# Second block of an attention and two-MLP kernel: the second weight tile's conversion queued on ScalarE behind the silu of tile (1,1)

## The chip, the cores and the metric

The kernel runs on one core of a Trainium2 chip. The metric is the device time of one execution in microseconds (us). Before the change three runs gave 1042.11, 1042.42 and 1044.66 us; the median is 1042.42 us.

## The reference

Three stages follow each other, all in float32 from outside:

```python
scores = scale * q @ k.T + (cum[:, None] - cum[None, :])   # causal, 4 batches x 8 heads x 576 rows x 64
x = softmax(scores) @ v                                    # reshaped to 2304 tokens x 512
xn = x / sqrt(mean(x * x) + 1e-6) * rms_g                  # first block
x = (silu(xn @ w_gate) * (xn @ w_val)) @ w_out             # 512 -> 1536 -> 512
h = x @ w_in                                               # second block
out = (silu(h)) @ w_out2                                   # 512 -> 2048 -> 512
```

`cum` is the running sum of log(f). The change touches the second block alone: `h = x @ w_in`, silu, and the product with `w_out2`.

## The kernel before, in words

**Numbers.** Every float32 operand of a large product is split into a high part (what ScalarE writes when it copies the value to the type fp32r, `hi`) and the rest (`lo`, value minus high part, computed on VectorE or GpSimd). A product is then three matmuls: high by high, low by high, high by low.

**Stages.** Attention comes first, then `layer("a", ...)` (the first block) for the first 1280 tokens and for the other 1024, then `layer("b", ...)` (the second block) for the same two parts, which the text calls the first and the second part of the second block. A layer walks over its inner dimension in groups of two 128-wide chunks (`for g in range(0, NF, G)`); the second block has eight groups in each part, called group 1 to group 8 here. In the first part they begin, with the first matmul that reads the operand `b11`, at 650.77, 674.75, 700.79, 728.35, 756.30, 782.40, 809.65 and 835.70 us of the profiled execution; the second part begins some 26 us after the last of these.

**One group.** Two chunks times two times 512 tokens make a 2 by 2 product that is computed with seven products instead of eight (the scheme of Winograd and Strassen). `Products` holds them: `p1` to `p7`, run in the order p1, p2, p6, p5, p7, p4, p3. Weight operands are `a11, a12, a21, a22` (pieces of the weights) and `s1` to `s4` (sums and differences of them); token operands are `b11, b21, b22` and `t1` to `t4`. Products p1, p6, p7 and p4 go to one PSUM bank, `u`, in which they accumulate. In between, ScalarE copies the bank out (`copy`, L731, tiles `c<-t`): after p1, after p6 and after p7. So p4's matmuls (`t<-t4h,wh` in the rows) can't start before the copy behind p7 is done. `plus` (L736, VectorE) adds a PSUM bank to such a copy. In the first part there is also a remainder of 256 tokens (`rest`).

Output tiles of a group are named by (chunk, token column). (1,1) is ready first after the seventh product, p7: copy of `u`, `plus`, then `out_` is called, which issues the silu (L829, ScalarE) and the split of its result into `hh` (L638, ScalarE) and `hl` (L639, VectorE). Then come the remainder's two tiles, (1,0) (behind p4) and (0,1) (behind p3). `hh` and `hl` are what the second product of the block (with `w_out2`) reads. That product is not run in its own group but in the next one: `second2` makes blocks of six matmuls, and the next group runs one or two of them behind each of its own products. Their PSUM tiles are `x` and `s`, and VectorE adds each to the result `xa` (L896).

**Weights of the second block.** `unit_in` (line 148) prepares a group's input weights while the group before it runs. Two tiles `f[0]` and `f[1]` come by DMA; GpSimd makes the four sums and differences (L162, `f<-f`, four instructions); ScalarE converts each tile to its high part (L165, `wh<-f`); the low part (L166, `wl<-f,wh`) is made by VectorE for the first tile, and for the second tile by GpSimd in the first part and by VectorE in the second part. The first tile holds a11, a12, s1 and s2 (for p1, p2, p6, p5), the second a21, a22, s3 and s4 (for p7, p4, p3).

```python
for i in range(2):
    u = slice(0 if plain or not i else 1, 4)
    nc.scalar.activation(out=hi[i][:, u], in_=f[i][:, u], func=AF.Copy)
    (nc.gpsimd if plain and i else nc.vector).tensor_tensor(out=lo[i][:, u], in0=f[i][:, u], in1=hi[i][:, u].bitcast(F32), op=ALU.subtract)
```

`plain` is true in the first part here. The weights arrive as 64-bit floats. In the first part the raw tile `st` is loaded (SyncE queue, L141) and unpacked to float32 by one ScalarE instruction (L143) and four of VectorE (L144 to L147), and the result is stored to DRAM (`kept`, L149) for the second part, which loads it ready-made (L134). Eight of the sixteen input tiles (those of groups 1, 2, 7 and 8) were unpacked during the first block; those of groups 3 to 6 are unpacked while groups 2 to 5 run. The output weights (`unit_out`, L193 on ScalarE and L194 on GpSimd, tiles `woh` and `wol`) are unpacked in every group of the first part. In groups 3 and 4 GpSimd also forms differences of the second part's tokens (L650).

**Order of the work.** A scheduler orders every engine's queue when the program is built, by readiness and priority; an engine then takes its queue strictly in order. `spread` (line 697) holds a unit back with `tc.issue_after(after)`: what is traced inside is queued on `after`'s engine somewhere behind the instruction `after`, without waiting for its end. For a unit of the second block `after` is one of the first silus of the group before (`marks`, `LEAD`).

Of the kernel before, what the change touches and what calls it, by code (L numbers as in the profile page):

```python
# [13 lines left out]
AF = mybir.ActivationFunctionType  # L14
# [47 lines left out]
def block_kernel(ctx: ExitStack, tc: tile.TileContext, q, k, v, f, w_gate, w_val, w_o1, rms_g, w_in, w_o2, ident_d, sel_d, hot_d, out):  # L62
    nc = tc.nc
# [56 lines left out]
    def plain_half():  # L120
        return stp.tile([P, 4, G2], F32, tag="f", name="f", bufs=3)

    def words(w):
        return (w, 1) if w.dtype == F32 else (w.bitcast(I32), 2)
# [26 lines left out]
    def unit_in(w, key, m, plain):  # L151


        w, s = words(w)
        hi, lo = zip(*((wip.tile([P, 4, G2], F32R, tag="wh", name="wh"), wip.tile([P, 4, G2], F32R, tag="wl", name="wl")) for _ in range(2)))
        f = [plain_half() for _ in range(2)]
        for i in range(2):
            weights(f[i][:, :2].rearrange("p a f -> p (a f)"), w[:, s * (m + i) * P : s * (m + i + 1) * P], s * P, (key, m + i))
        a11, a12, a21, a22 = f[0][:, 0], f[0][:, 1], f[1][:, 0], f[1][:, 1]
        s1, s2, s3, s4 = f[0][:, 3], f[0][:, 2], f[1][:, 2], f[1][:, 3]  # L160
        for out_, x, y, op in ((s1, a21, a22, ALU.add), (s2, s1, a11, ALU.subtract), (s3, a11, a21, ALU.subtract), (s4, a12, s2, ALU.subtract)):
            nc.gpsimd.tensor_tensor(out=out_, in0=x, in1=y, op=op)  # L162
        for i in range(2):
            u = slice(0 if plain or not i else 1, 4)
            nc.scalar.activation(out=hi[i][:, u], in_=f[i][:, u], func=AF.Copy)  # L165
            (nc.gpsimd if plain and i else nc.vector).tensor_tensor(out=lo[i][:, u], in0=f[i][:, u], in1=hi[i][:, u].bitcast(F32), op=ALU.subtract)  # L166
        ops = lambda i, b: tuple(t[i][:, b].rearrange("p (c f) -> p c f", f=P) for t in (hi, lo))
        return dict(a11=ops(0, 0), a12=ops(0, 1), s2=ops(0, 2), s1=ops(0, 3), a21=ops(1, 0), a22=ops(1, 1), s3=ops(1, 2), s4=ops(1, 3))
# [468 lines left out]
    def split(hi, lo, src):  # L637
        nc.scalar.activation(out=hi, in_=src, func=AF.Copy)  # L638
        nc.vector.tensor_tensor(out=lo, in0=src, in1=hi.bitcast(F32), op=ALU.subtract)  # L639
# [71 lines left out]
        with tc.issue_after(after):  # L711
            return fn(*args)

    places, marks, pending, done = [], [], [], [0]

    def terms(ps, abs_, start, stop):
        mms = [(a[i], b[j]) for a, b in abs_ for i, j in ((0, 0), (0, 1), (1, 0))]
# [91 lines left out]
    def layer(n, w_ins, w_out, second, ph, plain=False, ahead=()):  # L809
        NF = w_out.shape[0] // P  # L810
        in_fours[:] = [] if len(w_ins) == 2 and not plain else [True]
        G = 2
        for g in range(0, NF, G):
            win = [spread(*((unit_plain, w, f"{n}{z}", g) if plain else (unit_in, w, f"{n}{z}", g, ph == 0))) for z, w in enumerate(w_ins)]
            wout = [spread(unit_out, w_out, f"{n}o", m) for m in range(g, g + G)]
            for fn in ahead[g // G] if ahead else ():
# [8 lines left out]
            def out_(z, at_, a, w):  # L825
                psum_ = plain or at_ == (1, 0) or at_[1] == 2
                if z == 0:
                    hf = tmp.tile([P, TT], F32, tag="c", name="c")[:, :w] if psum_ else a
                    act = nc.scalar.activation(out=hf, in_=a, func=AF.Silu)  # L829
                    marks.append(act.ins)  # L830
                    if len(w_ins) == 2:
                        gates[at_] = hf
                        return
                else:
                    hf = gates[at_]
                    (nc.vector if psum_ or at_ == (0, 1) else nc.gpsimd).tensor_tensor(out=hf, in0=a, in1=hf, op=ALU.mult)  # L836
                few = dict(tag="r", bufs=2) if w < TT else dict(tag="h", bufs=5)
                hh, hl = (hp_.tile([P, w], F32R, tag=few["tag"] + p, name="h" + p, bufs=few["bufs"]) for p in "hl")
                split(hh, hl, hf)
                hs[at_] = hh, hl  # L840

            todo, pending[:] = list(pending), []
            order = group(win, out_, ph == 0, plain)

            if plain and coming:
# [110 lines left out]
```

## Time and profile before

| | us |
|---|---|
| median of the runs shown | 1042.42 |
| the profiled execution's own time | 1045.11 |
| its span | 1043.3 |
| TensorE (PE) busy in the span | 1023.5 (98%) |
| VectorE (DVE) busy | 763.2 (73%) |
| ScalarE (ACT) busy | 565.8 (54%) |
| GpSimd (POOL) busy | 411.8 (39%) |

The profile is one execution. The profiled execution took 2.69 us more than the median of the runs, and its span is 1.81 us shorter than its own time. All times in the rows are counted from the span's start. The granted clock of TensorE was 1.00 of full speed in every stretch of the second block, which is the 2.4 GHz level. "Busy" of TensorE is modelled, so it is not a sign of peak speed. A wait is named after the instruction that ended last before the waiting one could go on.

### The profile page before, as it was taken

To read this page: it belongs to the slowest core of one execution; us is meant where nothing else is said; L and a number is where in the kernel's file an instruction comes from. 1 tells how busy PE (TensorE), PEld (TensorE's weight loads), DVE (VectorE), ACT (ScalarE), POOL (GpSimd) and SP (SyncE) were. 2 spreads that over 40 slices of the span, in tenths; PEclk is the share of its full clock that TensorE was granted. 3 is DMA by queue.
4 is the path that set the end of the run, shared out by engine and by line. 5 is a ranking of instruction groups with operands and counts; after the bars stand their busy time and mean duration, and the time that the engine had idled before them with its cause. 6 is when DMAs were issued, how large, how long until landed. Compare 5 with 4: busy or idle time off the path is not lost.

```text
span 1043.3 us, 16043 instructions
## 1 busy us (share of the span) xinstructions
PE 1023.5 (98%) x5459; PEld 846.2 (81%) x5459; DVE 763.2 (73%) x1509; ACT 565.8 (54%) x1191; POOL 411.8 (39%) x601
## 2 busy tenths in 40 slices
PE   8999999999999999999999999999999999999998
PEld 7876777878788888888787787887788888888886
DVE  6889887877666767976478667968886696366664
ACT  6998988883442322543544455664454465544441
POOL 8786766511111216332355635235544323222300
PEclk8999999999999999999999999999999999999999
DMA  6564543113432424230433222134442233111102
GB/s 145 133 183 123 138 107 92 36 62 104 139 106 77 158 84 152 71 112 31 122 112 127 97 61 71 61 122 152 151 152 82 81 121 135 48 61 61 51 1 81
DMA packets 113010, 104.30 MB, mean 100 GB/s; under 512 B 62769, under 2 KB 83665, under 8 KB 112929
## 3 DMA queue, kind: packets, MB, share of 16 engines
q1 hardware_dynamic: 111200, 100.14, 31.6%
q10 hardware_dynamic: 1728, 3.15, 1.0%
q8 instruction: 43, 0.70, 0.3%
q14 instruction: 39, 0.31, 0.1%
HBM read 77.49 MB, written 25.76 MB: 99 GB/s over the span
## 4 chain that ended last, share of the span: by engine, by line
PE 78%; DVE 10%; ACT 4%; issue 3%; POOL 3%; DMA 1%; POOLq 0%; SPq 0%; DVEq 0%; ACTq 0%
PE t L719 33%; PE s L719 17%; PE x L719 13%; PE s L448 4%; PE o L500 4%; PE t L472 3%; POOL f L162 2%; DVE xa L896 1%; DVE hl L639 1%; ACT pr L463 1%; PE s L407 1%; DVE c L736 1%; DVE wl L166 1%; DVE f L146 1%; DVE c L147 1%
## 5 line engine op out<-in xcount | busy, mean ns | idle before, releaser
L194 POOL TENSOR_TENSOR wol<-c,woh 128x512 fp32r<-128x512 f32 x54 | 78.0, 1452 | 280.4 <-ACT woh L193 252.8
L639 DVE TENSOR_TENSOR hl<-c,hh 128x512 fp32r<-128x512 f32 (+1 forms) x140 | 110.4, 795 | 50.1 <-ACT hh L638 49.7
L162 POOL TENSOR_TENSOR f<-f 128x256 f32<-128x256 f32 x112 | 88.6, 812 | 132.9 <-DMA f<-keptb 67.0
L638 ACT ACTIVATE hh<-c 128x512 fp32r<-128x512 f32 (+1 forms) x140 | 79.5, 584 | 63.2 <-DVE c L836 27.0
L435 POOL TENSOR_SCALAR dt<-ncb,c8t 128x64 f32<-128x64 f32 (+2 forms) x144 | 79.8, 557 | 39.8 <-DVE nm L451 32.2
L731 ACT ACTIVATE c<-t 128x512 f32<-128x512 f32 x84 | 49.6, 591 | 71.6 <-PE t L719 71.2
L463 ACT ACTIVATE pr<-pr,nm 128x192 f32<-128x192 f32 (+3 forms) x144 | 80.2, 558 | 12.3 <-DVE nm L451 10.2
L829 ACT ACTIVATE c<-c 128x512 f32<-128x512 f32 x66 | 41.6, 630 | 80.0 <-DVE c L736 80.0
L166 DVE TENSOR_TENSOR wl<-f,wh 128x1024 fp32r<-128x1024 f32 (+1 forms) x48 | 61.1, 1281 | 30.8 <-ACT wh L165 30.8
L451 DVE CUSTOM_DVE_ANT_0 pr<-s,dt 128x256 f32<-128x256 f32 (+7 forms) x160 | 69.8, 451 | 17.3 <-PE s L448 6.1
L165 ACT ACTIVATE wh<-f 128x1024 fp32r<-128x1024 f32 (+1 forms) x56 | 54.1, 974 | 40.9 <-POOL f L162 21.2
L472 PE MATMUL t<-ident,pr 128*128 128x128 f32 x384 | 69.2, 280 | 2.3 <-ACT pr L463 1.6
L184 POOL TENSOR_TENSOR wl<-f,wh 128x1024 fp32r<-128x1024 f32 x12 | 28.7, 2395 | 94.5 <-ACT wh L183 94.5
L719 PE MATMUL s<-hh,woh 128*128 128x512 f32 (+1 forms) x172 | 64.2, 373 | 0.3 <-DVE xa L878 0.3
L719 PE MATMUL s<-hl,woh 128*128 128x512 f32 (+1 forms) x172 | 64.0, 372 | 0.0
L719 PE MATMUL s<-hh,wol 128*128 128x512 f32 (+1 forms) x172 | 64.0, 372 | 0.0
L736 DVE TENSOR_TENSOR c<-t,c 128x512 f32<-128x512 f32 x60 | 41.2, 687 | 30.5 <-ACT c L731 16.5
L829 ACT ACTIVATE c<-t 128x512 f32<-128x512 f32 (+1 forms) x74 | 37.6, 512 | 41.2 <-PE t L719 39.5
L896 DVE TENSOR_TENSOR xa<-x,xa 128x512 f32<-128x512 f32 x64 | 43.6, 681 | 21.3 <-PE x L719 21.2
L719 PE MATMUL x<-wol,hh 128*128 128x512 f32 (+1 forms) x146 | 57.0, 391 | 1.5 <-POOL wol L194 1.5
L878 DVE TENSOR_TENSOR xa<-s,xa 128x512 f32<-128x512 f32 (+1 forms) x72 | 45.6, 639 | 16.3 <-PE s L719 16.3
L719 PE MATMUL x<-woh,hh 128*128 128x512 f32 (+1 forms) x146 | 56.8, 389 | 0.0
(231 smaller groups left out, 3207.3 us busy)
## 6 DMA issues: line engine op xcount, KB each, us to landing
st<-in_moe_w_out_dram SPq DMA_DIRECT2D x28, 512.0 KB, 3.7
st<-in_moe_w_in_dram SPq DMA_DIRECT2D x16, 512.0 KB, 3.9
st<-in_moe_w_gate_dram SPq DMA_DIRECT2D x12, 512.0 KB, 3.9
kepta<-f SPq DMA_DIRECT2D x24, 256.0 KB, 2.3
st<-in_moe_w_val_dram SPq DMA_DIRECT2D x12, 512.0 KB, 4.5
f<-kepta SPq DMA_DIRECT2D x24, 256.0 KB, 2.7
f<-keptb SPq DMA_DIRECT2D x24, 256.0 KB, 2.6
out_dram<-xa SPq DMA_DIRECT2D x17, 256.0 KB, 2.0
```

The source lines that it names most:

```text
L162: nc.gpsimd.tensor_tensor(out=out_, in0=x, in1=y, op=op)
L165: nc.scalar.activation(out=hi[i][:, u], in_=f[i][:, u], func=AF.Copy)
L166: (nc.gpsimd if plain and i else nc.vector).tensor_tensor(out=lo[i][:, u], in0=f[i][:, u], in1=hi[i][:, u].bitcast(F32), op=ALU.subtract)
L194: nc.gpsimd.tensor_tensor(out=lo, in0=f, in1=hi.bitcast(F32), op=ALU.subtract)
L435: nc.gpsimd.tensor_scalar(out=dt, in0=p.nct[:, 0 if last else D :][:, :n], scalar1=c8t[:, c, p.i : p.i + 1], scalar2=1.0, op0=ALU.add, op1 ...
L451: nc.vector.tensor_tensor_reduce(out=self.pr[:, ks], in0=sp, in1=self.dt[:, ks], op0=ALU.add, op1=ALU.min, scale=-SCALE, scalar=3.0e38, ac ...
L463: e = nc.scalar.activation(out=pr, in_=pr, func=AF.Exp, bias=self.nm, scale=-1.0, accum_out=p.batch.sums[:, self.c, p.hp : p.hp + 1])
L472: nc.tensor.transpose(pt[:, jj * P : (jj + 1) * P], keys[:, jj * P : (jj + 1) * P], ident)
L638: nc.scalar.activation(out=hi, in_=src, func=AF.Copy)
L639: nc.vector.tensor_tensor(out=lo, in0=src, in1=hi.bitcast(F32), op=ALU.subtract)
L719: nc.tensor.matmul(ps, lhsT=l, rhs=r, start=start and z == 0, stop=stop and z == len(mms) - 1, skip_group_check=not (start and stop))
L829: act = nc.scalar.activation(out=hf, in_=a, func=AF.Silu)
```

## The change

The list `turned` remembers the last silu of a tile (1,1). The conversion of the second weight tile (`i` = 1) of the second block's input weights is now queued on ScalarE behind that silu. Nothing else is edited.

```diff
         for i in range(2):
             u = slice(0 if plain or not i else 1, 4)
-            nc.scalar.activation(out=hi[i][:, u], in_=f[i][:, u], func=AF.Copy)
+            with tc.issue_after(turned[0]) if i and key == "b0" and turned else ExitStack():
+                nc.scalar.activation(out=hi[i][:, u], in_=f[i][:, u], func=AF.Copy)
...
-    places, marks, pending, done = [], [], [], [0]
+    places, marks, pending, done, turned = [], [], [], [0], []
...
                     marks.append(act.ins)
+                    if at_ == (1, 1):
+                        turned[:] = [act.ins]
```

When group n's weights are prepared, the last silu of (1,1) that has been traced is that of group n-1, the group that runs meanwhile. The edit adds two lines ahead of most of the code, so a line number of before is one to three lower than that of the change (L165 is L166, L638 is L639, L731 is L732, L829 is L830).

TensorE's order is the same in both. The order changes on ScalarE, and where the scheduler's answer to that reaches GpSimd, VectorE and the SyncE queue.

ScalarE in group 3 of the first part, around the conversion of group 4's weights (`wh_8538` and `wh_8540`), the copy behind p7 (`c_8463<-t_8332`), and the silu and split of (1,1). Before:

```order
L165 ACTIVATE wh_8538<-f_8542 128x1024
L165 ACTIVATE wh_8540<-f_8543 128x1024
L731 ACTIVATE c_8463<-t_8332 128x512
L829 ACTIVATE c_8463<-c_8463 128x512
L638 ACTIVATE hh_8467<-c_8463 128x512
L829 ACTIVATE c_8492<-t_8479 128x256
L829 ACTIVATE c_8512<-t_8332 128x512
L638 ACTIVATE hh_8401<-c_8399 128x256
L638 ACTIVATE hh_8514<-c_8512 128x512
L638 ACTIVATE hh_8494<-c_8492 128x256
L193 ACTIVATE woh_8318<-c_8320 128x512
```

After:

```order
L166 ACTIVATE wh_8538<-f_8542 128x1024
L732 ACTIVATE c_8463<-t_8332 128x512
L830 ACTIVATE c_8463<-c_8463 128x512
L166 ACTIVATE wh_8540<-f_8543 128x1024
L639 ACTIVATE hh_8467<-c_8463 128x512
L830 ACTIVATE c_8492<-t_8479 128x256
L830 ACTIVATE c_8512<-t_8332 128x512
L639 ACTIVATE hh_8401<-c_8399 128x256
L639 ACTIVATE hh_8514<-c_8512 128x512
L639 ACTIVATE hh_8494<-c_8492 128x256
L194 ACTIVATE woh_8318<-c_8320 128x512
```

The second conversion went from the place ahead of the copy behind p7 to the place between the silu of (1,1) and its split `hh`. Groups 4 and 5 have the same picture. VectorE's and GpSimd's queues in groups 3 to 5 keep their order.

ScalarE in group 2 of the first part, around the conversion of group 3's weights (`wh_8272`, `wh_8274`). Before:

```order
L165 ACTIVATE wh_8274<-f_8277 128x1024
L894 ACTIVATE xa_64<-x_8183 128x512
L731 ACTIVATE c_8197<-t_8079 128x512
L829 ACTIVATE c_8197<-c_8197 128x512
L894 ACTIVATE xa_64<-s_8205 128x512
L638 ACTIVATE hh_8201<-c_8197 128x512
L829 ACTIVATE c_8226<-t_8213 128x256
L894 ACTIVATE xa_64<-x_8232 128x512
```

After:

```order
L897 ACTIVATE xa_64<-x_8183 128x512
L732 ACTIVATE c_8197<-t_8079 128x512
L830 ACTIVATE c_8197<-c_8197 128x512
L897 ACTIVATE xa_64<-s_8205 128x512
L639 ACTIVATE hh_8201<-c_8197 128x512
L830 ACTIVATE c_8226<-t_8213 128x256
L166 ACTIVATE wh_8274<-f_8277 128x1024
L897 ACTIVATE xa_64<-x_8232 128x512
```

Here the conversion lands behind the split of (1,1) and behind the silu of the remainder's second tile.

GpSimd at the passage from the first block's last group to group 1: the low part of group 1's second weight tile is `wl_7817`. Before:

```order
L166 TENSOR_TENSOR wl_7817<-f_7819,wh_7816 128x1024
L194 TENSOR_TENSOR wol_7572<-c_7573,woh_7571 128x512
L162 TENSOR_TENSOR f_8039<-f_8040 128x256
L162 TENSOR_TENSOR f_8040<-f_8039,f_8040 128x256
L162 TENSOR_TENSOR f_8039<-f_8039 128x256
L162 TENSOR_TENSOR f_8040<-f_8039 128x256
L836 TENSOR_TENSOR c_7739<-c_7749,c_7739 128x512
```

After:

```order
L195 TENSOR_TENSOR wol_7572<-c_7573,woh_7571 128x512
L162 TENSOR_TENSOR f_8039<-f_8040 128x256
L162 TENSOR_TENSOR f_8040<-f_8039,f_8040 128x256
L162 TENSOR_TENSOR f_8039<-f_8039 128x256
L162 TENSOR_TENSOR f_8040<-f_8039 128x256
L839 TENSOR_TENSOR c_7739<-c_7749,c_7739 128x512
L167 TENSOR_TENSOR wl_7817<-f_7819,wh_7816 128x1024
```

The low part went behind the output weights, the four sums of group 2's weights and the product of gate and value. In the second part the conversion moves in the same way on ScalarE, and its low part on VectorE; some loads on the SyncE queue change places (the even weight tiles' loads go behind the two loads of output weights).

## Rows read from the trace of the kernel before

**Rows 1.** Busy time by stretch: groups 2, 3, 4 and 6; last, most of group 4

```profile
core 0: us, PE busy (x) PEld busy (x) DVE busy (x) ACT busy (x) POOL busy (x), PEclk, DMA share, GB/s
674.75:700.79 26.04, 26.04 (x127) 22.01 (x126) 16.71 (x27) 17.51 (x34) 7.40 (x7) 1.00 0.38 122
700.79:728.35 27.56, 26.33 (x127) 21.94 (x126) 23.48 (x36) 12.87 (x24) 14.49 (x11) 1.00 0.43 144
728.35:756.30 27.95, 26.39 (x128) 21.86 (x126) 24.12 (x38) 12.94 (x24) 15.06 (x11) 1.00 0.41 141
...
782.40:809.65 27.25, 26.33 (x127) 21.94 (x126) 18.82 (x30) 11.96 (x22) 11.02 (x10) 1.00 0.25 78
...
726.17:747.90 21.73, 21.73 (x105) 18.15 (x104) 21.59 (x33) 9.15 (x18) 10.20 (x7) 1.00 0.35 119
```

**Rows 2.** Who waited for whom, PE from 617 us on

```profile
PE t L719 <- ACT c L731: 3.1, 3, 1.6
PE x L719 <- POOL wol L194: 1.5, 2, 0.9
```

**Rows 3.** Timeline of PE: start, duration, instruction, [idle before and its releaser]

```profile
724.14 0.50 PE L719 MATMUL t<-t4h,wh 128*128 128x512 f32 x1 [1.23 <-ACT c L731]
...
730.88 0.40 PE L719 MATMUL x<-woh,hl 128*128 128x512 f32 x1
...
752.08 0.50 PE L719 MATMUL t<-t4h,wh 128*128 128x512 f32 x1 [1.56 <-ACT c L731]
...
778.32 0.39 PE L719 MATMUL t<-t4h,wh 128*128 128x512 f32 x1
...
785.75 0.50 PE L719 MATMUL x<-wol,hh 128*128 128x512 f32 x1 [0.92 <-POOL wol L194]
```

**Rows 4.** Timeline of ACT in group 3

```profile
721.60 2.00 ACT L165 ACTIVATE wh<-f 128x1024 fp32r<-128x1024 f32 x2 [6.77 <-POOL f L162]
723.51 0.58 ACT L731 ACTIVATE c<-t 128x512 f32<-128x512 f32 x1
724.84 0.63 ACT L829 ACTIVATE c<-c 128x512 f32<-128x512 f32 x1 [0.76 <-DVE c L736]
725.51 0.63 ACT L638 ACTIVATE hh<-c 128x512 fp32r<-128x512 f32 x1
...
727.92 0.63 ACT L193 ACTIVATE woh<-c 128x512 fp32r<-128x512 f32 x1
```

**Rows 5.** Timeline of POOL in groups 3 to 5

```profile
723.68 2.49 POOL L166 TENSOR_TENSOR wl<-f,wh 128x1024 fp32r<-128x1024 f32 x1 [1.29 <-ACT wh L165]
...
747.38 2.95 POOL L162 TENSOR_TENSOR f<-f 128x256 f32<-128x256 f32 x4 [4.56 <-DVE f L147]
...
777.43 2.50 POOL L166 TENSOR_TENSOR wl<-f,wh 128x1024 fp32r<-128x1024 f32 x1 [1.30 <-ACT wh L165]
780.47 3.76 POOL L162 TENSOR_TENSOR f<-f 128x256 f32<-128x256 f32 x4 [0.53 <-DMA f<-keptb]
```

**Rows 6.** Timeline of DVE in groups 3 and 4

```profile
722.69 1.22 DVE L166 TENSOR_TENSOR wl<-f,wh 128x1024 fp32r<-128x1024 f32 x1 [2.74 <-ACT wh L165]
724.12 0.69 DVE L736 TENSOR_TENSOR c<-t,c 128x512 f32<-128x512 f32 x1 [0.20 <-ACT c L731]
...
726.17 0.69 DVE L639 TENSOR_TENSOR hl<-c,hh 128x512 fp32r<-128x512 f32 x1 [0.77 <-ACT hh L638]
...
728.32 1.02 DVE L639 TENSOR_TENSOR hl<-c,hh 128x256 fp32r<-128x256 f32 x2
...
731.03 0.75 DVE L145 TENSOR_SCALAR c<-c 128x512 int32<-128x512 int32 x2
...
```

**Rows 7.** Timeline, DVE and POOL in the same time, before group 1

```profile
641.47 2.69 DVE L639 TENSOR_TENSOR t1l<-xa,t1h 128x512 fp32r<-128x512 f32 x1
...
641.21 2.40 POOL L166 TENSOR_TENSOR wl<-f,wh 128x1024 fp32r<-128x1024 f32 x1 [8.76 <-ACT wh L165]
```

**Rows 8.** Timeline of POOL: low part of the output weights, group 3's begin

```profile
701.12 1.30 POOL L194 TENSOR_TENSOR wol<-c,woh 128x512 fp32r<-128x512 f32 x1 [4.25 <-ACT woh L193]
```

## The prediction

> **What bounds the kernel now.** I read the busy time by stretch first. TensorE is busy for nearly all of every group of the second block, so only a stretch longer than its busy time can give or take anything. A group without a stall takes 26.04 us; groups 3, 4 and 6 take 27.56, 27.95 and 27.25 [rows 1]. Next, who waited for whom: TensorE waited mainly for the copies L731 and for the output weights' low part, L194 [rows 2]. The timeline places the waits: 1.23 us ahead of p4 in group 3 (724.14), 1.56 ahead of p4 in group 4 (752.08), and 0.92 ahead of the first matmul with `wol` in group 6 (785.75) [rows 3]. In group 5 p4 starts at 778.32 with no stall.
>
> Why p4 waits is seen on ScalarE: two conversions, together 2.00 us, start at 721.60, when GpSimd's sums are there, and the copy behind p7 starts behind both, at 723.51 [rows 4]. So ScalarE gets the sums late, and the copy pays for both conversions.
>
> How late the sums are is set by VectorE. From 726.17 to 747.90 it is busy for 21.59 of 21.73 us [rows 1], and at the end of that, at 747.38, GpSimd starts the sums, released by VectorE's unpacking L147 [rows 5]. From there a chain runs: sums, first conversion, copy behind p7, p4. Hence in groups 3 and 4 a delay of VectorE behind tile (1,1) comes out, undiminished, at p4 of the next group.
>
> **What the change gives.** One conversion lasts 2.00 - 0.96 = 1.04 us and occupies ScalarE for (723.51 - 721.60) / 2 = 0.96. Without the second one ahead of it, the copy starts at 722.55, and p4 comes up to 0.96 earlier in each of groups 3 and 4. Group 5 has nothing to gain. Upper end: 2 x 0.96 = 1.9 us.
>
> **What it costs on ScalarE.** The conversion now stands between the silu of (1,1) and `hh`. `plus` needs the copy, but on VectorE it is behind the low part of the first weight tile, which ends at 722.69 + 1.22 = 723.91 [rows 6]; so it gains only some 0.28 (724.12 to 723.84), and the silu goes from 724.84 to 724.56. It ends at 725.19; ScalarE's instructions overlap by some 0.09 (723.60 against 723.51 [rows 4]), so the conversion starts at 725.10 and `hh` at 726.06 instead of 725.51: **+0.55**. Everything behind it on ScalarE (the remainder's silus and splits, `woh`, the unpacking L143) shifts by as much.
>
> **What it costs on GpSimd and VectorE.** GpSimd's low part of the second tile starts 0.08 after its conversion ends (723.68 against 723.60), now at 726.14 + 0.08, about 726.2 instead of 723.68: **+2.52**. Before, it ran while VectorE did `plus`, which reads a PSUM bank, and ended at 726.17, just when VectorE's `hl` of (1,1) started [rows 5, 6]. Now the two want to run in the same time. What that does, one place shows: at 641.21 GpSimd starts a like low part, at 641.47 VectorE starts a subtraction of two SBUF operands, and this takes 2.69 us, ending 0.55 after GpSimd's [rows 7], where the same shape takes 0.69 [rows 6]. The subtraction was stopped, while GpSimd's took 2.40, no longer than elsewhere.
>
> I carry that over. The 2.49 us of the low part hold 0.23 of waiting for VectorE's low part (from 723.68 to 723.91), so it lasts 2.26 and ends at 728.46. `hl` of (1,1) wants to start at 726.69 and ends at 728.46 + 0.55 = 729.01 instead of 726.86: +2.15. `woh` is then made from 728.47 to 729.1, and its low part, 1.30 us where nothing disturbs it [rows 8], runs until 730.45 and holds the remainder's `hl`, which ends at 730.73. The `hl` of (1,0), which ended at 728.32 + 1.02 = 729.34, comes at 732.26: +2.92. VectorE's backlog has some small gaps to take up; its L145, at 731.03 before, stands at 733.5. **So VectorE's loop shifts by +2.45 per group.** The lower bound, if nothing is held, is the 0.55 of ScalarE; the upper bound is 2.92. I take the value worked out from the row that resembles it most [rows 7].
>
> The Trainium skill's page "SBUF — State Buffer", section "SBUF: two separate sides", states the same: a VectorE instruction with two SBUF operands and a GpSimd instruction share a port pair as an exclusive lock, and whoever starts first holds it for its whole instruction. [...]
>
> The other consumer of a late `hl` is TensorE itself: in the next group its sixth matmul of the pending second product reads `hl` of (1,0) at 730.88 [rows 3]. At 732.26, with 0.09 for the passage, it waits **1.47**, in groups 4 and 5.
>
> **Elsewhere.** In groups 1 and 2 the conversion lands behind `hh`, so `hl` of (1,1) is not held; only the remainder's tiles can be, and group 2's VectorE is busy for 16.71 of 26.04 [rows 1]. Between 0 and 2.45 I take a shift of 0.8 for VectorE's loop into group 3. In the second part both low parts are VectorE's, so nothing of GpSimd can hold it, and ScalarE has room: 0. The loads that change places on the SyncE queue there are issued a group ahead: 0, and if that cover went, one load's wait at a group's start.
>
> **The sum**, as shifts against the profiled execution:
> - Group 3, p4: -0.96 + 0.8 = -0.16.
> - Group 4, start: the lateness of `hl` counts from VectorE, +0.8 + 1.47 = +2.27.
> - Group 4, p4: the chain gives -0.96 + 0.8 + 2.45 = +2.29; TensorE itself arrives 2.27 later. Part of the stall before p4 is thus spent earlier: +2.3.
> - Group 5, start: the loop is now at 0.8 + 2.45 = 3.25, and with 1.47, +4.7. Its p4 follows at 778.32 + 4.7; the copy is ready then, by about half a us.
> - Group 6, start: in group 5 GpSimd's low part was at 777.43, then four sums, 3.76 us [rows 5], then `wol`, for which TensorE waits at 785.75. The low part goes +2.52 later; its ending without the wait (0.23) and the gap of 0.53 behind it give some back, `hl` ahead of it takes 0.55: +2.3 on top of a loop now at 0.8 + 2 x 2.45 = 5.7. In all **+8.0**.
> - From group 6 on VectorE is busy for 18.82 of 27.25 [rows 1], and the next weights need no unpacking; what is late there is caught up. No more and nothing back.
>
> 1045.11 + 8.0 = 1053.1 for the profiled execution, which lies 2.69 above the median of the runs shown: **1050.4 us**. A measurement of this kernel can tell some 0.3%, 3.13 us, from no change: 1039.3 to 1045.55 is "same".
>
> **Rivals.**
> *Less is held (0.20).* The one place at 641 us is a single coincidence, and GpSimd might be held as often as VectorE: L194 after it is an instruction of two operands too, and VectorE's `hl` there may come first. If `hl` loses nothing, what is left is 0.55 per loop, twice, and the 2.3 of GpSimd's late chain ahead of group 6, while group 3's and 4's gain shrinks into them: about +3.4, 1045.8. For it: GpSimd has 10.20 us in 21.73 [rows 1], thus room. Against it: 2.69 where 0.69 is usual [rows 7].
>
> *Not slower (0.15).* The mechanism is which of the two gets to its operands first behind `hh`. If `hl` of (1,1) starts ahead of GpSimd's low part (this decides at 726.2 against 726.69; half a us on ScalarE is enough), GpSimd waits instead and VectorE loses only 0.55, which the earlier copy more than covers; and GpSimd's four sums, 3.76 us in group 5 against 2.95 in group 4 [rows 5], get back what they lost to VectorE. Both stalls then shrink by 0.96: 1042.42 - 1.9 = 1040.5. For it: the stalls and their cause are plain [rows 3, 4]. Against it: by the rows GpSimd is ready first.
>
> *More is held (0.08).* If in groups 1 and 2 the whole 2.45 is lost as well, and `wol` collides again, 2 to 3 us come on top: 1053.
>
> *The edit does nothing (0.05).* The order shows the move, so only the gain and the costs could cancel: 1042.4.
>
> **How the numbers follow.** The forecast itself has 0.52. The range, 1041.5 to 1053.0, holds it with its bounds (the shift in groups 1 and 2 at 0 gives 1049.6 or less; a loop of 1.5 in place of 2.45 about 1047.5), the first rival and half of the third, and leaves out the "not slower" case. Slower by over 0.3%: the forecast, half of the first rival, the third, 0.70. Within 0.3%: the other half, most of "not slower", and no effect, 0.26. Faster: 0.04, if the gain of 1.9 comes with GpSimd's recovery ahead of group 6.
>
> **What would show it.** Right: the copy behind p7 starts some 0.9 earlier behind the first conversion in group 3; GpSimd's low part starts at about 726; the `hl` of (1,1) beside it takes over 2 us; the sums in group 4 start over 2 us later than at 747.38; TensorE gets new waits for `hl` among the first matmuls of groups 4 and 5, and a wait for `wol` of 0.9 or more at group 6. Wrong: an `hl` of 0.7 us, VectorE with gaps in 726 to 748, or sums that start no later. Then the time lies at 1046 or below.

## The result and the profile after

The changed kernel takes 1054.05 us, the median of six runs (1052.57 to 1056.03). The kernel before, with three more runs, is at 1044.10 (1042.11 to 1047.34). The ratio is 1.0094, with a 95% interval from 1.0081 to 1.0107: **some 9.8 us slower**. The profiled execution's span is 1052.2 us against 1043.3.

First, who waited for whom: TensorE from 617 us on, in the profile after. The columns are total us, times, longest.

```profile
PE x L720 <- POOL wol L195: 5.6, 3, 4.4
PE t L720 <- ACT c L732: 3.4, 2, 1.8
PE x L720 <- DVE hl L640: 1.9, 2, 1.3
```

Against [rows 2]: the waits for the copy, which the change was to shorten, total 3.4 us, not less than the 3.1 of before. The waits for `wol` went from 1.5 to 5.6, and waits for `hl` are new. TensorE's timeline after says where:

```profile
722.22 0.50 PE L720 MATMUL t<-t4h,wh 128*128 128x512 f32 x1 [1.67 <-ACT c L732]
...
729.50 0.51 PE L720 MATMUL x<-wol,hh 128*128 128x512 f32 x1 [0.64 <-POOL wol L195]
731.32 0.50 PE L720 MATMUL x<-woh,hl 128*128 128x512 f32 x1 [1.31 <-DVE hl L640]
752.85 0.55 PE L720 MATMUL t<-t4h,wh 128*128 128x512 f32 x1 [1.77 <-ACT c L732]
761.95 0.50 PE L720 MATMUL x<-woh,hl 128*128 128x512 f32 x1 [0.62 <-DVE hl L640]
792.57 0.79 PE L720 MATMUL x<-wol,hh 128*128 128x512 f32 x1 [4.44 <-POOL wol L195]
```

The waits ahead of p4 (722.22 and 752.85) are 1.67 and 1.77 instead of 1.23 and 1.56 [rows 3]. Next, the stretches of groups 3 to 6, then four pieces of groups 4 and 6; the columns are those of [rows 1], with the granted clock third from the end.

```profile
698.42:726.44 28.02, 26.35 (x128) 21.95 (x126) 22.73 (x34) 11.55 (x21) 13.03 (x11) 1.00 0.43 141
726.44:758.68 32.24, 28.52 (x128) 22.99 (x126) 27.17 (x37) 14.41 (x28) 15.40 (x12) 0.95 0.36 122
758.68:785.70 27.02, 26.40 (x127) 21.86 (x126) 21.42 (x37) 11.18 (x21) 6.99 (x7) 1.00 0.42 137
785.70:818.78 33.08, 28.64 (x128) 23.62 (x126) 24.61 (x34) 13.61 (x27) 13.49 (x13) 0.90 0.22 72
...
752.85:755.00 2.15, 2.15 (x6) 1.71 (x7) 1.92 (x3) 0.80 (x2) 0.00 (x0) 0.57 0.40 164
755.00:757.00 2.00, 2.00 (x7) 1.57 (x6) 0.67 (x1) 2.00 (x5) 1.14 (x1) 0.61 0.00 0
792.50:795.00 2.50, 2.43 (x6) 1.95 (x7) 2.50 (x6) 0.23 (x1) 0.02 (x1) 0.50 0.00 0
795.00:797.00 2.00, 2.00 (x6) 1.51 (x5) 1.48 (x4) 0.63 (x1) 0.39 (x1) 0.50 0.14 54
```

The four groups take 120.36 us instead of 108.86: 11.5 more. The profile after is 2.37 us ahead where group 3 begins; 1.55 of that is there 24 us after the start, long before anything that the change touches, so it is no gain of the change: between 10 and 20 us the granted clock is 0.83 in this profile and 0.66 in that of before. The waits above sum to 10.45 us, those of before to 3.71: 6.74 more. **The other 4.8 us are no waits.** In groups 4 and 6 the granted clock fell to the lower of its two levels, 1.2 GHz, at the waits of 1.77 and 4.44: to 0.50 in the pieces from 792.50 to 797, and in group 6 it was at 0.50 from 791 to 792 already, while TensorE still waited. A group's length less 26.04 and less its waits is 2.48 in group 4 (0.35 before) and 2.60 in group 6 (0.29 before). Where the clock stays at 1.00, some 0.3 us is left over for each wait (0.29 to 0.35 in the groups of before with one, 0.90 in group 4 of the run low_dve with three). So the clock took about 1.6 us in group 4 and 2.3 in group 6; the rest comes with the two further waits.

Last, the timeline of ScalarE, GpSimd and VectorE in groups 3 to 5 of the kernel after:

```profile
720.62 1.06 ACT L166 ACTIVATE wh<-f 128x1024 fp32r<-128x1024 f32 x1 [7.27 <-POOL f L162]
721.59 0.58 ACT L732 ACTIVATE c<-t 128x512 f32<-128x512 f32 x1
...
725.06 0.62 ACT L639 ACTIVATE hh<-c 128x512 fp32r<-128x512 f32 x1
...
725.23 2.40 POOL L167 TENSOR_TENSOR wl<-f,wh 128x1024 fp32r<-128x1024 f32 x1 [3.84 <-ACT wh L166]
...
725.71 2.48 DVE L640 TENSOR_TENSOR hl<-c,hh 128x512 fp32r<-128x512 f32 x1 [1.57 <-ACT hh L639]
...
748.33 0.68 DVE L147 SCALAR_TENSOR_TENSOR f<-st,f 128x512 int32<-128x512 int32 x1
...
776.96 0.68 DVE L147 SCALAR_TENSOR_TENSOR f<-st,f 128x512 int32<-128x512 int32 x1
```

The copy starts 0.97 behind the first conversion, as the change wants. GpSimd's low part ends at 727.63, and VectorE's `hl` beside it takes 2.48 us instead of 0.69 [rows 6] and ends at 728.19, 0.56 after it. That is the hold that the forecast took from [rows 7]. The same 2.48 stands in groups 4 and 5.

### The profile page after: what moved, and what is told of

It is laid out like the page before. It is cut to its first block, busy times and chain, and to the rows that moved or that the text cites. A ratio compares the mean times of both kernels' runs of the same rounds, so it can differ in the third digit from the quotient of the medians.

```text
span 1052.2 us, 16038 instructions
## 1 busy us (share of the span) xinstructions
PE 1025.9 (98%) x5459; PEld 846.9 (80%) x5459; DVE 770.5 (73%) x1509; ACT 564.0 (54%) x1191; POOL 408.5 (39%) x601
## 4 chain that ended last, share of the span: by engine, by line
PE 75%; DVE 10%; ACT 5%; issue 5%; POOL 3%; DMA 2%; POOLq 0%; DVEq 0%; ACTq 0%
PE t L720 32%; PE s L720 16%; PE x L720 12%; PE s L449 5%; PE o L501 4%; PE t L473 3%; POOL f L162 2%; DMA st<-in_moe_w_in_dram 1%; DVE hl L640 1%; DVE wl L167 1%; PE s L408 1%; ACT pr L464 1%; DVE c L737 1%; DVE xa L899 1%; DVE pr L452 1%
## 5 line engine op out<-in xcount | busy, mean ns | idle before, releaser
L640 DVE TENSOR_TENSOR hl<-c,hh 128x512 fp32r<-128x512 f32 (+1 forms) x140 | 126.7, 913 | 42.1 <-ACT hh L639 39.8
L639 ACT ACTIVATE hh<-c 128x512 fp32r<-128x512 f32 (+1 forms) x140 | 79.3, 582 | 59.5 <-DVE c L839 26.9
L732 ACT ACTIVATE c<-t 128x512 f32<-128x512 f32 x84 | 49.6, 591 | 77.2 <-PE t L720 76.8
L830 ACT ACTIVATE c<-c 128x512 f32<-128x512 f32 x66 | 41.6, 630 | 89.8 <-DVE c L737 89.7
L464 ACT ACTIVATE pr<-pr,nm 128x192 f32<-128x192 f32 (+3 forms) x144 | 80.2, 558 | 11.5 <-DVE nm L452 9.5
L166 ACT ACTIVATE wh<-f 128x1024 fp32r<-128x1024 f32 (+1 forms) x56 | 54.4, 973 | 41.9 <-POOL f L162 22.8
L830 ACT ACTIVATE c<-t 128x512 f32<-128x512 f32 (+1 forms) x74 | 37.4, 509 | 40.5 <-PE t L720 39.2
L720 PE MATMUL x<-woh,hl 128*128 128x512 f32 (+1 forms) x146 | 57.0, 391 | 1.9 <-DVE hl L640 1.9
```

The source lines that it names most:

```text
L464: e = nc.scalar.activation(out=pr, in_=pr, func=AF.Exp, bias=self.nm, scale=-1.0, accum_out=p.batch.sums[:, self.c, p.hp : p.hp + 1])
L720: nc.tensor.matmul(ps, lhsT=l, rhs=r, start=start and z == 0, stop=stop and z == len(mms) - 1, skip_group_check=not (start and stop))
```

## The experiments

The theory, H: GpSimd's late low part holds VectorE's `hl`, and the loop of VectorE's unpacking, GpSimd's sums, first conversion, copy and p4 hands the delay on from group to group. Rivals are that the loss comes from ScalarE's order alone (O), or from the places that the change also moves in other groups and in the second part (E). Every kernel is compared with runs of the kernel before on the same chip.

| run | median, us | ratio to before, interval |
|---|---|---|
| only_345 | 1054.01 | 1.0102, 1.0086 to 1.0117 |
| twice | 1051.25 | 1.0075, 1.0057 to 1.0092 |
| hh_late | 1048.17 | 1.0044, 1.0029 to 1.0059 |
| pieces_345 | 1052.18 | 1.0076, 1.0059 to 1.0092 |
| low_dve | 1048.59 | 1.0046, 1.0028 to 1.0064 |
| copy_first | 1047.36 | 1.0032, 1.0019 to 1.0046 |
| copy_pieces | 1047.33 | 1.0038, 1.0025 to 1.0050 |
| both_behind | 1046.75 | 1.0017, 1.0008 to 1.0027 |
| free_copy | 1049.76 | 1.0069, 1.0056 to 1.0081 |
| low_late | 1051.48 | 1.0082, 1.0069 to 1.0095 |
| low_ahead_hl | 1044.38 | 1.0000, 0.9989 to 1.0012 |
| low_behind_out | 1041.49 | 0.9983, 0.9974 to 0.9992 |

**Where: groups 3 to 5 alone (only_345).**

```diff
-            with tc.issue_after(turned[0]) if i and key == "b0" and turned else ExitStack():
+            with tc.issue_after(turned[0]) if i and key == "b0" and plain and m in (6, 8, 10) and turned else ExitStack():
```

> The change in groups 3 to 5 of the first part alone (three conversions moved instead of all of them); order elsewhere as before. Theory H (GpSimd's late low part holds VectorE's hl, VectorE's loop of unpacking, sums, conversion, copy carries the delay on): hl of (1,1) in groups 3, 4, 5 takes about 2.5 us again; the stall before p4 of group 3 falls from 1.23 to about 0.3; the sums of group 5 start some 2.7 later and those of group 6's weights some 5.4; total some 6 to 9 us over before, about 1051.5. Rival E (the moves elsewhere, in groups 1, 2, 6, 7 and in the second part, carry the loss): within 2 us of before, about 1044.

Here `m` is the first chunk of the group whose weights are prepared: 6, 8 and 10 are groups 4 to 6, so the conversions that move lie in groups 3 to 5. The whole loss is there, 1054.01, so E falls. This kernel has no delay from group 2, and is the clean measure of the forecast's terms. Its timeline in groups 3 to 5, then its stretches of groups 4 to 6 and four us of group 4:

```profile
725.97 2.41 POOL L167 TENSOR_TENSOR wl<-f,wh 128x1024 fp32r<-128x1024 f32 x1 [3.83 <-PE s L720]
726.44 2.48 DVE L640 TENSOR_TENSOR hl<-c,hh 128x512 fp32r<-128x512 f32 x1 [1.57 <-ACT hh L639]
...
730.22 0.50 PE L720 MATMUL x<-wol,hh 128*128 128x512 f32 x1 [0.64 <-POOL wol L195]
732.04 0.79 PE L720 MATMUL x<-woh,hl 128*128 128x512 f32 x1 [1.32 <-DVE hl L640]
...
748.76 0.68 DVE L147 SCALAR_TENSOR_TENSOR f<-st,f 128x512 int32<-128x512 int32 x1
...
777.07 0.68 DVE L147 SCALAR_TENSOR_TENSOR f<-st,f 128x512 int32<-128x512 int32 x1
```

```profile
727.15:757.50 30.35, 28.35 (x128) 22.93 (x127) 25.90 (x37) 12.84 (x25) 14.38 (x12) 0.94 0.38 130
757.50:787.66 30.16, 28.20 (x127) 23.12 (x126) 25.06 (x38) 14.69 (x28) 10.03 (x9) 0.94 0.37 123
787.66:818.20 30.54, 27.96 (x128) 23.11 (x127) 22.56 (x33) 11.99 (x22) 12.15 (x12) 0.94 0.23 78
732.00:736.00 4.00, 3.96 (x11) 3.17 (x12) 4.00 (x9) 1.64 (x3) 0.00 (x0) 0.60 0.00 0
```

Group 3 begins 0.22 earlier than before (700.57 against 700.79). Counted from there, `hl` of (1,1) starts 0.49 later than before and ends 2.28 later: 0.49 is ScalarE's order, 1.79 the hold. VectorE's last unpacking is 2.36 later in group 4 (748.76 against 746.62 - 0.22) and 4.86 in group 5 (777.07 against 772.43 - 0.22). That is 2.36 and 2.50 a group, where the forecast had 2.45. The wait of p4 in group 3 is down to 0.25 us, and p4 of group 4 does not wait at all.

What was not expected is the size, 10.6 us over before instead of 6 to 9. The waits of groups 3 to 6 sum to only 6.74 us (0.25, 0.64 + 1.32, 0.64 + 1.31, 2.58), 3.0 more than before. But each of groups 4, 5 and 6 has a stretch at the lower clock (mean 0.94, 0.60 in the four us behind the wait at 732.04): length less 26.04 and less waits is 2.35, 2.17 and 1.92. With 0.3 for each wait taken off, 4.9 us are the clock's, more than half of the 8.8 by which the four groups are longer than before.

**GpSimd late, ScalarE untouched (twice); `hh` late, GpSimd untouched (hh_late).**

```diff
+            for _ in range(2 if plain and i and key == "b0" and m in (6, 8, 10) else 1):
-            (nc.gpsimd if plain and i else nc.vector).tensor_tensor(...)
+                (nc.gpsimd if plain and i else nc.vector).tensor_tensor(...)
```

> The kernel before, ScalarE's order untouched, but GpSimd computes the low part of the second tile twice in groups 3 to 5 (the same values written again), so that the second one runs at 726 to 728.5, where the change puts it. Theory H: the second low part runs beside hl of (1,1) or beside the next splits, one of them takes over 2 us, VectorE's loop shifts by 2 to 3 us a group, total 6 to 12 us over before, 1050 to 1056. Rival O (the loss comes from ScalarE's order: hh and all that stands behind it there start 0.5 to 1 us later): nothing changes on ScalarE, so within 1 us of before, 1044.

```diff
+                if n == "b" and ph == 0 and g in (4, 6, 8) and at_ == (1, 1):
+                    for _ in range(2):
+                        nc.scalar.activation(out=hh, in_=hf, func=AF.Copy)
                 split(hh, hl, hf)
```

> The kernel before with hh of (1,1) in groups 3 to 5 written three times on ScalarE (the same values), so that hl comes about 1 us later as with the change, while the conversions and GpSimd's low part stay where they were. Theory H: hl takes its usual 0.69, VectorE's loop shifts by at most 1 us a group, total 0 to 3 us over before, about 1046. Rival O: as much as the change, 8 to 10 us over before, about 1053.

With nothing moved on ScalarE, the doubled low part costs 7.8 us, as H has it. The timeline of twice in group 3 (the two low parts are one row):

```profile
724.33 0.69 DVE L640 TENSOR_TENSOR hl<-c,hh 128x512 fp32r<-128x512 f32 x1 [0.77 <-ACT hh L639]
724.94 0.69 DVE L897 TENSOR_TENSOR xa<-x,xa 128x512 f32<-128x512 f32 x1
725.54 2.03 DVE L640 TENSOR_TENSOR hl<-c,hh 128x256 fp32r<-128x256 f32 x1
...
721.83 5.45 POOL L167 TENSOR_TENSOR wl<-f,wh 128x1024 fp32r<-128x1024 f32 x2 [1.29 <-ACT wh L165]
```

`hl` of (1,1) came first this time, took its 0.69, and it was GpSimd that waited: its second low part, from 724.42 on, took 2.87 instead of 2.41. The next split, half as wide and usually 0.41, then took 2.03, while `xa` ahead of it, which reads a PSUM bank, kept its 0.69 beside GpSimd. So it is whoever starts first, as in the forecast's "not slower" rival; GpSimd's next instruction was just as harmful.

In hh_late `hl` is not held, as expected, but the run is 4.6 us slower, not 0 to 3. Its timeline in group 3 shows why:

```profile
726.03 0.69 DVE L639 TENSOR_TENSOR hl<-c,hh 128x512 fp32r<-128x512 f32 x1 [2.22 <-ACT hh L638]
...
728.17 2.10 DVE L639 TENSOR_TENSOR hl<-c,hh 128x256 fp32r<-128x256 f32 x2
...
728.21 1.51 POOL L194 TENSOR_TENSOR wol<-c,woh 128x512 fp32r<-128x512 f32 x1 [3.64 <-ACT woh L193]
```

With the silu of the remainder between its copies, `hh` came 1.7 later, not 1, and the last splits (the remainder's second and that of (1,0)) ran into the low part of the output weights: 2.10 instead of 1.02 [rows 6]. VectorE's last unpacking in group 4 is 2.59 later (747.33 against 746.62 - 1.88), nearly the sum of these two delays, 1.7 and 1.1. So O is not nothing: what ScalarE delays before a split goes into the loop, about 0.5 a group in the change. The wait of p4 in group 4 was 2.72, and that group, 31.87 us long, has another 2.5 that is no wait, with a granted clock of 0.95.

**A shorter hold (pieces_345) and none (low_dve).** Both are only_345 with one more edit for m in (6, 8, 10).

```diff
-            (nc.gpsimd if plain and i else nc.vector).tensor_tensor(out=lo[i][:, u], ...)
+                for k in range(4):
+                    nc.gpsimd.tensor_tensor(out=lo[i][:, k], ...)
```

> As only_345, but GpSimd makes the low part of the second tile in four instructions of a quarter each. Theory H (VectorE's hl is stopped until the end of the GpSimd instruction that runs, plus 0.55): hl of (1,1) waits for one piece instead of the whole, so it takes about 1.2 us instead of 2.5; VectorE's loop loses about 1 us a group less; about 1049 to 1051, against 1054.0 for only_345. Rival O (ScalarE's later hh is the cost): ScalarE is as in only_345, so 1054 again. Rival S (the two engines share, in proportion to what each moves): the same work overlaps, so hl takes as long in sum, 1053 to 1054.

```diff
-            (nc.gpsimd if plain and i else nc.vector).tensor_tensor(...)
+            (nc.gpsimd if plain and i and not (key == "b0" and m in (6, 8, 10)) else nc.vector).tensor_tensor(...)
```

> As only_345, but VectorE makes the low part of the second tile in groups 3 to 5, ahead of hl of (1,1), so that GpSimd is idle while the splits run. VectorE has 1.14 us more to do a group. Theory H: hl takes its usual 0.69 and starts about 0.7 later than in the kernel before; VectorE's loop shifts by some 0.7 to 1.5 a group; GpSimd's chain ahead of group 6 is free of the low part; total 0 to 4 us over before, about 1045.5. Rival O: ScalarE as in only_345, and VectorE has even more to do: 1054 or above.

Group 3 and the stretch of group 6 of pieces_345, then the same of low_dve:

```profile
724.17 3.75 POOL L169 TENSOR_TENSOR wl<-f,wh 128x256 fp32r<-128x256 f32 x4 [3.82 <-ACT wh L166]
724.65 0.81 DVE L644 TENSOR_TENSOR hl<-c,hh 128x512 fp32r<-128x512 f32 x1 [1.57 <-ACT hh L643]
...
784.23:815.03 30.80, 27.93 (x127) 23.08 (x126) 23.10 (x30) 11.93 (x22) 11.92 (x12) 0.94 0.23 78
```

```profile
725.35 0.69 DVE L640 TENSOR_TENSOR hl<-c,hh 128x512 fp32r<-128x512 f32 x1
...
782.85:812.05 29.20, 26.33 (x127) 21.94 (x126) 21.11 (x34) 13.73 (x26) 12.98 (x12) 1.00 0.26 82
```

Pieces: the `hl` of (1,1) took 0.81 us, so VectorE gets in between two GpSimd instructions, which rival S doesn't give; against O the time alone decides little, as the intervals of this run and of only_345 overlap. But now GpSimd is held up too: the four pieces take 3.75 us instead of 2.41. One that meets nothing takes 0.74, so four would take some 2.96; the other 0.8 is waiting for VectorE (the second piece, beside `hl`, took 1.20). The low part of the output weights comes later, and TensorE waits for it 1.81, 1.86 and 2.87 at the heads of groups 4 to 6. The clock falls in groups 5 and 6 (0.94 over each). 1052.2 is a miss of the range by 1 us: the collision was passed on, not removed.

low_dve: `hl` takes 0.69, and the loss falls from only_345's 10.6 us to 4.8, which O can't explain (0 to 4 was expected); but the last splits still meet the output weights' low part (1.85), p4 of group 4 waits 1.72, and TensorE waits 2.87 for the `wol` of group 6. On GpSimd that stands behind the four sums of group 7's weights, which begin 3.5 later than before, counted from group 3, released by a load that was issued at 779.41, right behind VectorE's later low part of the first tile, and take 4.41 instead of 3.76 [rows 5]. The clock stayed at 1.00 in all four groups of its profile.

**The conversion a place earlier (copy_first, copy_pieces), or both conversions behind the copy (both_behind).** In the first two, `turned` holds the copy of p7 instead of the silu, for m in (6, 8, 10); in the third the first conversion goes there too.

```diff
                 self.u3 = copy(self.u)
+                turned[:] = latest
```

> The kernel before, but the second conversion in groups 3 to 5 goes behind the copy of p7 and ahead of the silu of (1,1), where ScalarE waits for plus anyway. Theory H: p4 comes up to 0.96 earlier in groups 3 and 4 (stalls of about 0.3 and 0.6 instead of 1.23 and 1.56), hh and hl no later than before, GpSimd's low part 0.5 later, so that it holds hl by 0.5 at most: 0 to 2 us under before, about 1043. Rival O': any conversion that moves behind the copy delays what follows on ScalarE and costs the gain again: 1 to 3 us over before, about 1046.

> As copy_first (second conversion behind the copy of p7, ahead of the silu; it gave 1047.4), but with GpSimd's low part in four pieces. Theory H: hl of (1,1), which took 1.23 there, takes under 1.0; the later low part of the output weights still stops the remainder's split (1.94 there); about 1 us better than copy_first, 1045 to 1047. Rival: nothing gained, 1047.4.

> Both conversions of groups 3 to 5 queued behind the copy of p7, so that the copy, and with it p4, no longer waits for VectorE's unpacking and GpSimd's sums at all. Theory H: the waits of p4 for the copy in groups 3 and 4 (1.23, 1.56) go; but GpSimd's low part comes about 2 us later than in the kernel before and stops hl or the remainder's splits for 1 to 2 us a group, which shows at the head of the next group (waits for hl) and at group 6 (wait for wol, 2 to 4 us): 1044 to 1050, about 1047. Rival O: hh starts no later than before, so only the gain of 2.8 remains: 1041.

copy_first is a miss: 3 to 4 us slower, not up to 2 faster. The copy was early (0.25 wait in group 3), but GpSimd's low part, now 1.72 ahead of VectorE's `hl` instead of 2.49 (721.37 and 723.09 there), held it so that it took 1.23, and the low part of the output weights held the last splits (1.94). In the kernel before, GpSimd's low part fits between the splits to the hundredth: it ends at 726.17, where `hl` starts [rows 5, 6]. Less than a us breaks that. The wait for `wol` in group 6 is 2.40 there, with a granted clock of 0.94 over the group. Rival O' comes near in time, not in cause: counted from the group's begin, that `hl` started 0.31 earlier than before, so ScalarE did not delay it. copy_pieces gave nothing over it: there the last splits take 2.11.

both_behind separates the hold from the loop. Its timeline in group 3, and its stretches of groups 3 to 5:

```profile
722.44 2.41 POOL L167 TENSOR_TENSOR wl<-f,wh 128x1024 fp32r<-128x1024 f32 x1 [1.82 <-ACT wh L166]
722.91 2.49 DVE L640 TENSOR_TENSOR hl<-c,hh 128x512 fp32r<-128x512 f32 x1 [0.76 <-ACT hh L639]
```

```profile
699.07:725.11 26.04, 26.04 (x128) 22.02 (x126) 23.36 (x31) 12.75 (x24) 14.41 (x11) 1.00 0.46 152
725.11:752.23 27.12, 26.34 (x128) 21.94 (x126) 24.09 (x37) 11.29 (x21) 12.97 (x11) 1.00 0.42 146
752.23:782.45 30.22, 28.21 (x127) 23.13 (x126) 27.11 (x42) 14.77 (x29) 11.53 (x11) 0.94 0.41 131
```

`hl` is held as long as in the change, yet p4 no longer waits in groups 3 to 6, because the copy stands ahead of both conversions and so no longer waits for VectorE's unpacking. Left are waits for `hl` and `wol` at the heads of groups 4 to 6 (0.78; 0.69 and 1.31; 0.71, the last expected at 2 to 4) and one stretch at the lower clock in group 5. In the change itself, groups 6 and 7 say the same: `hl` takes 2.47 there too, at 814.21 and 840.25, and groups 7 and 8 last 26.04.

**A version that beats both (free_copy, low_late, low_ahead_hl, low_behind_out).** All take GpSimd's low part of the second tile out of the splits: VectorE makes the second tile's low part in groups 3 to 5. They differ in the place of that instruction. free_copy and low_late put it behind the split of (1,0), with the conversions behind the copy or left free; low_ahead_hl right behind the first tile's low part; low_behind_out behind the unpacking of the output weights:

```diff
+            with tc.issue_after(turned[0]) if key == "b0" and plain and m in (6, 8, 10) and turned else ExitStack():
...
+            if late_low:
+                deferred.append(_p(nc.vector.tensor_tensor, ...))
...
             wout = [spread(unit_out, w_out, f"{n}o", m) for m in range(g, g + G)]
+            while deferred:
+                with tc.issue_after(lows[0]):
+                    deferred.pop()()
```

`lows` holds the last L147 of the output weights, `turned` the copy of p7.

> As both_behind (1046.8), but VectorE makes the low part of the second tile of groups 3 to 5, queued behind its split of tile (1,0), so that GpSimd no longer runs beside hl of (1,1). The scheduler also moves some conversions, unpackings and output-weight work on ScalarE and VectorE by a place or two. Theory H: no hl of (1,1) over 0.8 us in groups 3 to 5; no wait of p4 for the copy; the waits for hl at the head of groups 4 and 5 (0.78, 1.31) shrink; VectorE has 1.14 us more to do a group but nothing at p4 waits for its loop any longer; GpSimd's chain ahead of group 6 is shorter by 2.4; 2 to 4 us under before, about 1041. Rival B (VectorE's load alone is the bound): 1.14 us more a group shows in full, 1046 or above.

> The kernel before, but with the low part of the second tile of groups 3 to 5 on VectorE, behind its split of tile (1,0); the second conversion is bound to nothing, though the scheduler itself now puts it behind the copy or the silu in these groups, and in groups 4 and 5 the first one behind the copy too, as in free_copy. Theory H: as free_copy but for the stall before p4 of group 3: 1 to 3 us under before, about 1042. Rival B: 1046 or above.

> As low_behind_out, but VectorE makes the second tile's low part right behind the first one's, ahead of hl of (1,1). Nothing moves behind it but what VectorE does. Theory H: the splits come 1 us later than in low_behind_out and meet GpSimd's low part of the output weights; waits for hl of 0.4 to 1 us at the heads of groups 4 to 6; still no wait of p4 for the copy: 1 to 3 us under before, about 1041.5. Rival B: 1045 or above.

> As free_copy (both conversions of groups 3 to 5 behind the copy of p7, the second tile's low part on VectorE), but that low part stands behind the unpacking of the output weights instead of ahead of it; free_copy, at 1049.8, had groups 3 and 4 without a stall (26.04 and 26.10 us) and lost its time where TensorE waited for late output weights in groups 5 and 6. Theory H: groups 3 to 5 at 26.0 to 26.5 us each, group 6 with a wait for wol of 1 us at most: 2.5 to 4 us under before, about 1040. Rival B (VectorE has no room for 1.14 us more a group): waits for wol or for the first tile's low part at the heads of groups 5 and 6 again, 1045 or above.

free_copy and low_late missed: groups 3 and 4 of free_copy last 26.04 and 26.10, no `hl` of (1,1) is held, but the scheduler let the low part go ahead of the output weights' unpacking, and TensorE waited for `woh` and `wol` 2.7 us in group 5 and 4.1 in group 6, with the lower clock in both (low_late: 2.7 and 3.9). In low_behind_out the low part stands behind that unpacking, and little else changes places; its stretches of groups 3 to 6:

```profile
698.89:724.93 26.04, 26.04 (x127) 22.02 (x126) 23.38 (x35) 12.73 (x24) 12.02 (x10) 1.00 0.46 152
724.93:751.11 26.18, 26.18 (x128) 21.94 (x127) 23.80 (x36) 11.54 (x21) 13.35 (x10) 1.00 0.43 151
751.11:778.53 27.42, 26.33 (x127) 21.94 (x126) 24.29 (x41) 14.75 (x28) 7.98 (x9) 1.00 0.41 135
778.53:806.01 27.48, 26.33 (x127) 21.94 (x126) 21.70 (x31) 11.81 (x22) 10.65 (x10) 1.00 0.27 87
```

**1041.49 us, 0.9983 of the kernel before** (0.9974 to 0.9992). Left are waits for `wol` of 1.09 and 1.15 in groups 5 and 6. The gain, 1.9, is less than the 2.5 to 4 expected, mostly because of the one in group 5; 1 us in group 6 was allowed for. low_ahead_hl, where the splits come later, is no better than before, where 1 to 3 under was expected: its last splits meet GpSimd's low part of the output weights (1.87 in group 3), and the wait for `wol` in group 6 is 2.10, with a granted clock of 0.94 over the group.

## Why the prediction was wrong

The direction and the chain were right, the size was not: 1054.05 lies above the range's end at 1053.0. Part of that is the base. The forecast put +8.0 on a profiled execution taken to be 2.69 above the median; with six runs the median before is 1044.10, and the measured difference is 9.8. So of the 3.65 us by which the result lies above the forecast some 1.7 are the base and some 2.0 the sum. The rest, step by step, in the profile after, counted from group 3's begin (2.37 earlier than before):

- *The gain.* Right: the copy starts 0.97 behind the first conversion, and only_345 shows the wait of p4 in group 3 at 0.25.
- *"+0.55" on ScalarE.* Right: 0.49 in only_345.
- *The hold.* Right: 2.48 us, ending 0.56 after GpSimd, whose low part took 2.40, not the 2.26 of the forecast.
- *"VectorE's loop shifts by +2.45 per group."* Right where nothing comes before it: 2.36 and 2.50 in only_345. In the change it was 2.68 and 2.82.
- *"Between 0 and 2.45 I take a shift of 0.8 for VectorE's loop into group 3."* Too small. It was 1.40 (748.33's counterpart in group 3 stands at 717.70, against 718.67 - 2.37). GpSimd's low part ran from 695.79 to 698.19 and the low part of the output weights from 698.90 to 700.24, both beside splits, and three of these took 3.50 us instead of 1.55. So p4 of group 3, forecast at -0.16, came at +0.45: the gain was gone in the first group. It is not what made the loss too large: only_345 has no such shift and is as slow.
- *"At 732.26 ... it waits 1.47, in groups 4 and 5."* It waited 0.64 and 1.31 in group 4, since `wol` was late too, and 0.62 in group 5.
- *"In all +8.0" at the wait for `wol` in group 6.* It was +9.19 (792.57 against 785.75 - 2.37).
- *"No more and nothing back" from group 6 on.* **This step failed.** Group 7 starts +11.50 later, 2.3 us more than at that wait, because TensorE ran at the lower clock behind it. In group 4 the shift grew from 3.14 at p4 to 4.75 at the group's end in the same way, by 1.6. The sum had no term for the clock, it put what TensorE loses behind a wait at nothing; the clock had been 1.00 in every stretch of the second block before. It should have been a rival with a price, which the rows now give: 1.6 and 2.3 us. The Trainium skill's page "TensorE: Matmul & The Clock Gate", section "HAM oscillation — how this bites in real kernels", tells of a kernel whose matmuls start at the lower clock behind each wait for a DMA; the trace agrees that this can happen (0.50 from 792.50 to 797).

When exactly the clock falls stays open. It did at waits of 1.77 and 4.44, and in only_345 at 0.64 and 1.32 in short succession; it did not at 1.67 in group 3, nor at 0.64 and 1.31 in group 4 of the change. The length of the wait does not tell: at the head of group 6 TensorE waited 2.87 us in pieces_345 and in low_dve, and the clock fell in the first (0.94 over the group) and stayed at 1.00 in the second; in twice it stayed at 1.00 behind 2.71 in group 4. No run here tells these apart. Without the 3.9 us of the clock the four groups would be 7.6 longer than before, near the forecast's 8.0. Part of that is luck, since the waits at the heads of groups 4 and 5 were 1.95 and 0.62 in place of 1.47 each. Time lost to the clock may also let VectorE's loop catch up, which no run shows by itself, so waits and clock can't be taken off one by one.

Of the rivals, "less is held" named 1045.8 and is out by the rows; "not slower" had the right condition, who starts first, and copy_first and twice show that moving one instruction makes the next pair collide. "More is held" named 1053, nearest to the result; part of it came true, 1.40 from group 2 in place of 0.8, but by only_345 the size isn't owed to that.

## What to carry to other kernels

Where VectorE and GpSimd both work on SBUF operands, a tuned order has their instructions interleaved; before an instruction is moved on a third engine, look at what its consumer on GpSimd will run beside, and count every VectorE instruction with two SBUF operands there at GpSimd's remaining time and some half a us. If that VectorE work belongs to a loop that the bottleneck waits for, the loss is paid once a group and is handed on; cutting the loop (here: the copy ahead of both conversions) was worth more than making one of its steps shorter. And new waits of TensorE are to be priced with the clock that may fall at them, here 1.6 us a time or more, not by their length alone.

## What was not expected of the hardware

- A held VectorE instruction ends sooner after GpSimd's than its own duration: 0.54 to 0.56 us after for one that takes 0.69 (in the change, only_345 and both_behind), 0.29 for one that takes 0.41 (twice: 727.57 against 727.28). The page "SBUF — State Buffer" of the Trainium skill, section "A bandwidth-pool intuition that's wrong (but worth ruling out)", has a DMA that GpSimd issues go on about 115 ns past VectorE's end. No run here shows that case; carried over to VectorE behind GpSimd, and with the whole duration behind it, the first would end 0.8 after by an estimate, and by the rows it ends 0.25 sooner.
- The hold works both ways, and a GpSimd instruction waits for VectorE as VectorE does for it: of the four pieces of GpSimd's low part in pieces_345 the first took 0.74 us and the second, which met `hl`, 1.20; together they took 3.75, where four times 0.74 is 2.96.
- The clock of TensorE, at 1.00 at all waits of up to 1.56 us in the second block of the kernel before, fell to half at several of these, and cost 1.6 to 2.3 us a time in the change. The same wait of 2.87 us went with and without it.
